# Expert layers in units of 384 tokens over two batches, with the second layer's operands swapped

## The chip, the cores and the metric

One core of a Trainium2 chip runs the kernel in one launch. The metric is the device time of that launch in microseconds; the kernel before has a median of 549.85 us over three runs (548.9 to 550.44).

## What is computed

Attention with two kinds of sparse windows over 8 batches of 576 tokens, and behind it a gated two-layer network on each batch. Everything is float32.

```python
# q, k, v: (8 batches, 8 heads, 576 tokens, 64); windows of 32 keys, heads 4..7 with every fourth key of 128
scores = q @ k.T / 8, masked;  attn = softmax(scores);  a = attn @ v
x = a as (8, 576, 512)
h = relu(x @ w_in)                              # 512 -> 1024
conv = sum over k of conv_w[k] * h[token + k - 1]   # three tokens, zero outside a batch
out = (h * sigmoid(conv)) @ w_out               # 1024 -> 512
```

The weights come in as float64 and are split in the kernel.

## The kernel before, in words

Precision is had by splitting: x, the gated h (called g) and both weights are kept as a high part and a low part, each in the type that TensorE multiplies in one go (written `F32R`), and a product is three matmuls (`TERMS`): high by high, low by high, high by low.

**Attention** (`attention`, four calls for each batch, one for each pair of heads). A call is: load q and k (tile `qk`) and v on SP's queue; scores on TensorE (L248) into the one `att` slot of PSUM; mask, maximum, subtraction on VectorE (L254, L257, L260, L262); the exponential on ScalarE (L264); sum, reciprocal, scaling and a 32x32 transpose into `pt` on VectorE (L266 to L273); the product with v on TensorE (L283), again into `att`. ScalarE copies the product into the high part of x (L320). In the first two batches TensorE subtracts it (L327, L330) and ScalarE copies the low part; later VectorE makes the low part (L335).

**Weights** (`weights`). Sixteen chunks of 512 columns and a small one for the convolution are rebuilt from the float64 words by VectorE (L430 to L441), after a first step on ScalarE (L428). Ten of the sixteen are finished by TensorE with three matmuls of 512 columns (L450 in float32, L451 and L452), the others by VectorE (L457, L463). The chunks pass through the three `out` buffers.

**The two layers** (`expert`, one call for each batch). The first layer has weights stationary and 288 tokens moving (L353): 8 chunks of 128 hidden units by 2 halves of the batch by 4 pieces of x by 3 terms, 192 matmuls. ScalarE's relu writes both halves into one `h` tile of 576 tokens and two zero columns (L360). The gating of a chunk is then one copy with the middle tap on ScalarE (L371), two taps on VectorE (L365), the sigmoid on ScalarE (L376), the product on VectorE (L378), the high part on ScalarE (L380) and the low part on VectorE (L382). There are three `h` and three `c` tiles and one `g` for each chunk. The second layer again has weights stationary and 288 tokens moving (L395), 192 matmuls, and writes the output transposed; ScalarE copies it out of PSUM (L402) and SP stores it. The host turns the result round.

**What sets the order.** `Planner` holds every piece of work as a task with an engine, a cost, what it comes after, the buffers it uses and a due time. `order()` goes through the tasks by list scheduling: on the engine that can start first, of the tasks that could start within 0.25 us the one with the earliest due time is taken. The program is then issued in that order, and each engine runs its own instructions strictly in it. Due times come from tables (`DUE`, `PAIR`, `WI`, `WO`).

Of the kernel before, what the change touches and what calls it, by code (L numbers as in the profile page):

```python
# [55 lines left out]
ONE = dict(start=True, stop=True, skip_group_check=True)  # L56

# [100 lines left out]
def attn_moe(ctx: ExitStack, tc: tile.TileContext, qk_p, qk_d, v_p, v_d, w_in, w_out, conv, mask, out):  # L158
# [10 lines left out]
    wo = [[const.tile([128, 512], F32R, name=f"wo{j}{c}") for c in range(2 * NC)] for j in range(2)]  # L169
# [172 lines left out]
    def expert(b, ready, wired, wored, conved):  # L342
        due, gated, out_due = DUE[b]
        x = [xs[b, p] for p in range(NP)]
        h, c, g = ([Buffer(n) for _ in range(NF)] for n in "hcg")
        relu = []
        for u in range(2 * NF):
            fc, hf = u // 2, u % 2
            ps, last = Buffer("nn" if b == 0 and u % 4 > 1 else "mm"), None

            def first(fc, hf, ps, k):
                for i, (jw, jx) in enumerate(TERMS):
                    nc.tensor.matmul(ps.t[:, 0:HALF], wi[jw][fc][:, k * 128:k * 128 + 128],  # L353
                                     x[k].t[jx][:, hf * HALF:hf * HALF + HALF],
                                     start=(k == 0 and i == 0), stop=(k == NC - 1 and i == 2))

            for k in range(NC):
                last = plan.add("PE", 0.396, due + 1.6 * u + 0.4 * k, lambda a=(fc, hf, ps, k): first(*a),
                                [last, wired[fc], *(ready[k] if b == 0 else sum(ready, []))], [ps, x[k]], "E")
            relu.append(plan.add("ACT", 0.4, due + 1.6 * u + 1.6, lambda fc=fc, hf=hf, ps=ps: nc.scalar.activation(  # L360
                out=h[fc].t[:, 1 + hf * HALF:1 + hf * HALF + HALF], in_=ps.t[:, 0:HALF], func=AF.Relu),
                [last], [ps, h[fc]]))

        def tap(fc, k):
            nc.vector.scalar_tensor_tensor(out=c[fc].t, in0=h[fc].t[:, k:S + k], scalar=conv_sb[:, k, fc:fc + 1],  # L365
                                           in1=c[fc].t, op0=ALU.mult, op1=ALU.add)

        gates = []
        for fc in range(NF):
            d = gated + 3.2 * fc  # L370
            t = plan.add("ACT", 0.777, d, lambda fc=fc: nc.scalar.activation(  # L371
                out=c[fc].t, in_=h[fc].t[:, 1:S + 1], func=AF.Copy, scale=conv_sb[:, 1, fc:fc + 1]),
                [relu[2 * fc], relu[2 * fc + 1], conved], [h[fc], c[fc]])
            for k in (0, 2):
                t = plan.add("DVE", 0.815, d + 0.5, lambda fc=fc, k=k: tap(fc, k), [t], [h[fc], c[fc]])
            t = plan.add("ACT", 0.686, d + 1.0, lambda fc=fc: nc.scalar.activation(  # L376
                out=c[fc].t, in_=c[fc].t, func=AF.Sigmoid), [t], [c[fc]], "sigmoid")
            t = plan.add("DVE", 0.755, d + 1.5, lambda fc=fc: nc.vector.tensor_tensor(  # L378
                out=c[fc].t, in0=c[fc].t, in1=h[fc].t[:, 1:S + 1], op=ALU.mult), [t], [c[fc], h[fc]])
            hi = plan.add("ACT", 0.675, d + 2.0, lambda fc=fc: nc.scalar.copy(out=g[fc].t[0], in_=c[fc].t),  # L380
                          [t], [c[fc], g[fc]])
            lo = plan.add("DVE", 0.755, d + 2.5, lambda fc=fc: nc.vector.tensor_tensor(  # L382
                out=g[fc].t[1], in0=c[fc].t, in1=g[fc].t[0].bitcast(F32), op=ALU.subtract), [hi], [c[fc], g[fc]])
            gates.append(lo)

        for dm in range(NC):
            o = Buffer("out")
            outs = []
            for hf in range(2):
                u = 2 * dm + hf  # L390
                ps, last = Buffer("nn"), None

                def second(dm, hf, ps, k):
                    for i, (jw, jg) in enumerate(TERMS):
                        nc.tensor.matmul(ps.t[:, 0:HALF], wo[jw][2 * dm + k // 4][:, k % 4 * 128:k % 4 * 128 + 128],  # L395
                                         g[k].t[jg][:, hf * HALF:hf * HALF + HALF],
                                         start=(k == 0 and i == 0), stop=(k == NF - 1 and i == 2))

                for k in range(NF):
                    last = plan.add("PE", 0.396, out_due + 3.3 * u + 0.4 * k, lambda a=(dm, hf, ps, k): second(*a),  # L400
                                    [last, wored[2 * dm + k // 4], gates[k]], [ps, g[k]], "E")
                outs.append(plan.add("ACT", 0.4, out_due + 3.3 + 3.3 * u, lambda hf=hf, ps=ps, o=o: nc.scalar.copy(  # L402
                    out=o.t[:, hf * HALF:hf * HALF + HALF], in_=ps.t[:, 0:HALF]), [last], [ps, o]))
                if b == B - 1:
                    plan.add("SP", 0.6, out_due + 4.0 + 3.3 * u, lambda dm=dm, hf=hf, o=o: nc.sync.dma_start(
                        out=out[b, dm, :, hf * HALF:hf * HALF + HALF], in_=o.t[:, hf * HALF:hf * HALF + HALF]),
                        [outs[-1]], [o])
            if b < B - 1:
                plan.add("SP", 1.2, out_due + 4.0 + 6.6 * dm, lambda dm=dm, o=o: nc.sync.dma_start(
                    out=out[b, dm], in_=o.t[:, :S]), outs, [o])  # L410
# [156 lines left out]
```

## Time and profile before

| what | value |
|---|---|
| median of three runs | 549.85 us (548.9 to 550.44) |
| span of the profiled execution | 549.1 us |
| mean granted clock of TensorE | 0.990 |
| last matmul ends, last ScalarE copy ends | 545.6, 546.1 us |
| TensorE, VectorE, ScalarE busy | 522.4, 415.7, 298.1 us |
| matmuls of the first and of the second layer | 1536 and 1536, 288 columns each |
| DMA, mean over the span | 95 GB/s |

In the profile PE is TensorE, PEld its weight loads, DVE VectorE, ACT ScalarE, POOL GpSimd and SP the engine that issues the transfers. A row of a group of instructions holds line, engine, operation, what it writes and reads, shapes, count, then busy time and mean duration in ns, and the idle time of the engine just before. A matmul's duration holds the time it takes to run through the array, so matmuls that follow each other overlap; what one costs is the distance between two starts. The median of the runs is 0.75 us above the profiled span.

### The profile page before, as it was taken

To read this page: it belongs to the slowest core of one execution; us is meant where nothing else is said; L and a number is where in the kernel's file an instruction comes from. 1 tells how busy PE (TensorE), PEld (TensorE's weight loads), DVE (VectorE), ACT (ScalarE), POOL (GpSimd) and SP (SyncE) were. 2 spreads that over 40 slices of the span, in tenths; PEclk is the share of its full clock that TensorE was granted. 3 is DMA by queue.
4 is the path that set the end of the run, shared out by engine and by line. 5 is a ranking of instruction groups with operands and counts; after the bars stand their busy time and mean duration, and the time that the engine had idled before them with its cause. 6 is when DMAs were issued, how large, how long until landed. Compare 5 with 4: busy or idle time off the path is not lost.

```text
span 549.1 us, 19084 instructions
## 1 busy us (share of the span) xinstructions
PE 522.4 (95%) x8664; PEld 497.2 (91%) x8664; DVE 415.7 (76%) x695; ACT 298.1 (54%) x556; POOL 0.9 (0%) x12
## 2 busy tenths in 40 slices
PE   3499978999999999999999999999999999999997
PEld 2468876999999999999999999999989999999997
DVE  4968998899997389946998389946988389946920
ACT  2457784855752486337742486237742486337721
POOL 0000000000000000000000000000000000000000
PEclk9999996999999999999999999999999999999999
DMA  7756513331044102630055102530045102300011
GB/s 247 268 157 215 195 52 137 119 121 44 7 138 152 30 23 65 200 110 23 13 161 170 32 23 72 190 113 23 17 152 162 45 23 58 117 26 23 0 44 44
DMA packets 17072, 52.31 MB, mean 95 GB/s; under 512 B 2016, under 2 KB 3168, under 8 KB 16992
## 3 DMA queue, kind: packets, MB, share of 16 engines
q1 hardware_dynamic: 16848, 51.02, 27.8%
q8 instruction: 68, 1.11, 0.9%
q10 hardware_dynamic: 144, 0.08, 0.1%
q14 instruction: 12, 0.10, 0.1%
HBM read 41.66 MB, written 9.44 MB: 93 GB/s over the span
## 4 chain that ended last, share of the span: by engine, by line
PE 92%; DVE 3%; ACT 2%; DMA 2%; issue 1%; ACTq 0%
PE nn L395 38%; PE mm L353 35%; PE att L283 8%; PE att L248 6%; PE nn L450 2%; PE nn L353 2%; PE att L327 1%; DMA qk<-in_qk_d_dram 1%; DMA qk<-in_qk_p_dram 1%; PE nn L451 0%; PE nn L452 0%; DVE pt L273 0%; DVE s L271 0%; PE att L330 0%; DVE c L365 0%
## 5 line engine op out<-in xcount | busy, mean ns | idle before, releaser
L365 DVE SCALAR_TENSOR_TENSOR c<-h,conv_sb,c 128x576 f32<-128x576 f32 x128 | 103.9, 815 | 48.4 <-ACT c L371 46.9
L360 ACT ACTIVATE h<-mm 128x288 f32<-128x288 f32 x120 | 48.8, 408 | 50.4 <-PE mm L353 50.1
L402 ACT COPY out<-nn 128x288 f32<-128x288 f32 x64 | 25.5, 400 | 70.1 <-PE nn L395 66.1
L378 DVE TENSOR_TENSOR c<-c,h 128x576 f32<-128x576 f32 x64 | 47.6, 755 | 9.4 <-ACT c L376 7.8
L283 PEld LDWEIGHTS att<-pt,v 32*64 32x64 f32 x3072 | 40.8, 138 | 14.8 <-DVE s L257 4.6
L283 PE MATMUL att<-pt,v 32*64 32x64 f32 (+2 forms) x3072 | 44.2, 232 | 9.4 <-DVE s L257 3.5
L371 ACT ACTIVATE c<-h,conv_sb 128x576 f32<-128x576 f32 x64 | 49.7, 776 | 1.3
L248 PE MATMUL att<-qk 64*32 64x64 f32 x2432 | 36.2, 235 | 11.0 <-DMA qk<-in_qk_d_dram 5.5
L248 PEld LDWEIGHTS att<-qk 64*32 64x32 f32 x2432 | 30.2, 111 | 16.9 <-DMA qk<-in_qk_d_dram 5.5
L376 ACT ACTIVATE c<-c 128x576 f32<-128x576 f32 x64 | 42.5, 678 | 2.1 <-DVE c L365 1.6
L353 PE MATMUL mm<-x2a,wi 128*128 128x288 f32 x144 | 40.5, 296 | 0.0
L353 PE MATMUL mm<-x1a,wi 128*128 128x288 f32 x144 | 40.3, 296 | 0.0
L353 PE MATMUL mm<-x3a,wi 128*128 128x288 f32 x144 | 40.3, 295 | 0.0
L353 PE MATMUL mm<-x0a,wi 128*128 128x288 f32 x144 | 40.3, 295 | 0.0
L395 PE MATMUL nn<-g2a,wo 128*128 128x288 f32 x128 | 37.0, 304 | 0.0
L395 PE MATMUL nn<-g0a,wo 128*128 128x288 f32 x128 | 36.4, 299 | 0.2
L395 PE MATMUL nn<-g6a,wo 128*128 128x288 f32 x128 | 36.6, 299 | 0.0
L395 PE MATMUL nn<-g3a,wo 128*128 128x288 f32 x128 | 36.4, 299 | 0.0
L395 PE MATMUL nn<-g1a,wo 128*128 128x288 f32 x128 | 36.4, 299 | 0.0
L395 PE MATMUL nn<-g4a,wo 128*128 128x288 f32 x128 | 36.4, 299 | 0.0
L395 PE MATMUL nn<-g5a,wo 128*128 128x288 f32 x128 | 36.4, 299 | 0.0
L395 PE MATMUL nn<-g7a,wo 128*128 128x288 f32 x128 | 36.1, 300 | 0.1
(194 smaller groups left out, 1502.5 us busy)
## 6 DMA issues: line engine op xcount, KB each, us to landing
qk<-in_qk_d_dram SPq DMA_DIRECT2D x16, 664.0 KB, 4.4
qk<-in_qk_p_dram SPq DMA_DIRECT2D x16, 592.0 KB, 4.9
out_dram<-out SPq DMA_DIRECT2D x28, 288.0 KB, 2.2
v<-in_v_d_dram SPq DMA_DIRECT2D x16, 384.0 KB, 3.4
v<-in_v_p_dram SPq DMA_DIRECT2D x16, 384.0 KB, 3.5
out<-in_w_in_dram SPq DMA_DIRECT2D x8, 512.0 KB, 4.5
out<-in_w_out_dram SPq DMA_DIRECT2D x8, 512.0 KB, 4.2
out_dram<-out SPq DMA_DIRECT2D x8, 144.0 KB, 1.8
```

Source lines behind the costliest of these rows:

```text
L248: nc.tensor.matmul(sc.t[quad * 32:quad * 32 + 32, slot // 4, slot % 4 * W:slot % 4 * W + W], q, k, start=i == 0, stop=i == len(parts) - 1, ...
L283: nc.tensor.matmul(tv.t[hd * 64:hd * 64 + 64, bank, o:o + n], v.t[quad * 32:quad * 32 + 32, block // 2, block % 2 * 64:block % 2 * 64 + 64 ...
L327: nc.tensor.matmul(tv.t[:, t, 0:128], minus, main[:, t], start=False, stop=True, skip_group_check=True)
L353: nc.tensor.matmul(ps.t[:, 0:HALF], wi[jw][fc][:, k * 128:k * 128 + 128], x[k].t[jx][:, hf * HALF:hf * HALF + HALF], start=(k == 0 and i = ...
L360: relu.append(plan.add("ACT", 0.4, due + 1.6 * u + 1.6, lambda fc=fc, hf=hf, ps=ps: nc.scalar.activation(out=h[fc].t[:, 1 + hf * HALF:1 + ...
L365: nc.vector.scalar_tensor_tensor(out=c[fc].t, in0=h[fc].t[:, k:S + k], scalar=conv_sb[:, k, fc:fc + 1], in1=c[fc].t, op0=ALU.mult, op1=ALU ...
L371: t = plan.add("ACT", 0.777, d, lambda fc=fc: nc.scalar.activation(out=c[fc].t, in_=h[fc].t[:, 1:S + 1], func=AF.Copy, scale=conv_sb[:, 1, ...
L376: t = plan.add("ACT", 0.686, d + 1.0, lambda fc=fc: nc.scalar.activation(out=c[fc].t, in_=c[fc].t, func=AF.Sigmoid), [t], [c[fc]], "sigmoid")
L378: t = plan.add("DVE", 0.755, d + 1.5, lambda fc=fc: nc.vector.tensor_tensor(out=c[fc].t, in0=c[fc].t, in1=h[fc].t[:, 1:S + 1], op=ALU.mult ...
L395: nc.tensor.matmul(ps.t[:, 0:HALF], wo[jw][2 * dm + k // 4][:, k % 4 * 128:k % 4 * 128 + 128], g[k].t[jg][:, hf * HALF:hf * HALF + HALF], ...
L402: outs.append(plan.add("ACT", 0.4, out_due + 3.3 + 3.3 * u, lambda hf=hf, ps=ps, o=o: nc.scalar.copy(out=o.t[:, hf * HALF:hf * HALF + HALF ...
L450: nc.tensor.matmul(ps.t, ident, t(), start=True, stop=False)
```

## The change

The unit of the two layers is no longer a batch but 384 tokens: two batches of 576 tokens are three units, each of two segments of 192. x of both batches now lies in one tile for each pair of heads, the two batches side by side with zero columns before, between and behind (`xt`), instead of seven rotating buffers.

The first layer's moving operand is a window of two runs of 194 columns, a segment with a neighbour at each side, so 388 columns and no halves; relu writes both runs into `h` at once, and the neighbours are computed twice. The gating works on two runs of 192. There are 12 `g` buffers instead of 8, each of 384 tokens.

In the second layer g is stationary, 128 tokens at a time, and the weights move, 512 columns; the output comes out with tokens in rows, 36 stores of 128 rows. `w_out` is laid out by 128 hidden units instead of by output columns. GpSimd's memsets write the zero columns of x, 24 instead of 6.

All due times are new: a table `DUE` of its own for each unit, pair of heads and weight chunk. Costs of the planner's tasks follow the new shapes.

```diff
+UNITS = 3
+SEG, SEGS = S // 3, 2
+HALO = SEG + 2
+UNIT = SEGS * SEG
+XB = S + 1
+XW = 2 * XB + 2
...
+DUE = {
+    "first": (-267.74, -248.77, 696.14, -362.32, 670.22, 937.38, 948.43, 1088.83, 1172.91, 1498.80, 1690.92, 1705.61),
...
+}
...
-    slots("x", 7, [128, S], F32R, 2)
-    slots("g", NF, [128, S], F32R, 2)
-    hs = slots("h", 3, [128, S + 2])
-    slots("c", 3, [128, S])
+    xt = [[const.tile([128, XW], F32R, name=f"x{p}{'ab'[j]}") for j in range(2)] for p in range(NP)]
+    for p in range(NP):
+        for odd in range(2):
+            plan.pool(f"x{p}{odd}", [[t[:, 1 + odd * XB:1 + odd * XB + S] for t in xt[p]]])
+    slots("g", 12, [128, UNIT], F32R, 2)
+    slots("h", 3, [128, SEGS, HALO])
+    slots("c", 3, [128, SEGS, SEG])
...
+        def window(t):
+            at = [(s // 3) * XB + s % 3 * SEG for s in (part * SEGS, part * SEGS + 1)]
+            t = t[:, at[0]:at[1] + HALO]
+            return bass.AP(t.tensor, t.offset, [t.ap[0], [at[1] - at[0], SEGS], [1, HALO]])
...
-                    nc.tensor.matmul(ps.t[:, 0:HALF], wi[jw][fc][:, k * 128:k * 128 + 128],
-                                     x[k].t[jx][:, hf * HALF:hf * HALF + HALF],
+                    nc.tensor.matmul(ps.t[:, 0:SEGS * HALO], wi[jw][fc][:, k * 128:k * 128 + 128], window(xt[k][jx]),
                                      start=(k == 0 and i == 0), stop=(k == NC - 1 and i == 2))
...
-                last = plan.add("PE", 0.396, due + 1.6 * u + 0.4 * k, lambda a=(fc, hf, ps, k): first(*a),
+                last = plan.add("PE", 0.493, first_due + 1.97 * fc + 0.49 * k, lambda a=(fc, ps, k): first(*a),
...
-                        nc.tensor.matmul(ps.t[:, 0:HALF], wo[jw][2 * dm + k // 4][:, k % 4 * 128:k % 4 * 128 + 128],
-                                         g[k].t[jg][:, hf * HALF:hf * HALF + HALF],
-                                         start=(k == 0 and i == 0), stop=(k == NF - 1 and i == 2))
+                    nc.tensor.matmul(ps.t, g[k].t[jg][:, j * 128:j * 128 + 128], wo[jw][k],
+                                     start=(k == 0 and i == 0), stop=(k == NF - 1 and i == 2))
...
-                    last = plan.add("PE", 0.396, out_due + 3.3 * u + 0.4 * k, lambda a=(dm, hf, ps, k): second(*a),
+                last = plan.add("PE", 0.648, out_due + 5.2 * j + 0.65 * k, lambda a=(j, ps, k): second(*a),
...
-    for h, in hs:
-        nc.gpsimd.memset(h[:, 0:1], 0.0)
-        nc.gpsimd.memset(h[:, S + 1:S + 2], 0.0)
+    for p in range(NP):
+        for t in xt[p]:
+            for i in range(3):
+                nc.gpsimd.memset(t[:, i * XB:i * XB + 1].bitcast(F32), 0.0)
...
-        "w_out": w_out.reshape(2, 4, 128, NC, 128).transpose(3, 0, 2, 1, 4).reshape(2 * NC, 128, 512),
+        "w_out": w_out.reshape(NF, 128, DM),
```

In the changed kernel the lines are: scores L261, masks to transpose L267 to L286, product with v L296, subtraction on TensorE L340 and L343, low part of x on VectorE L348, first layer L373, taps L384, product L398, low part of g L402, second layer L411, weight splits L441 to L474 on VectorE and L461 to L463 on TensorE.

Where the instructions moved is seen at the ninth attention. First TensorE's order before around the ninth product with v (its rows end in the instruction's written shape); 384 matmuls of the first layer and 264 of the second stand ahead of it:

```order
L395 MATMUL nn_163<-g6a,wo_93 128x288
L395 MATMUL nn_163<-g7a,wo_85 128x288
L395 MATMUL nn_163<-g7b,wo_85 128x288
L395 MATMUL nn_163<-g7a,wo_93 128x288
L283 MATMUL att_159<-pt_112,v_102 64x32 x8
L283 MATMUL att_159<-pt_112,v_102 64x64 x24
L283 MATMUL att_159<-pt_112,v_102 64x32 x16
L395 MATMUL nn_162<-g0a,wo_84 128x288
```

That is the second layer of the second batch in full flow. In the changed kernel the same place in TensorE's order, with 252 matmuls of the first layer and 78 of the second ahead of it:

```order
L373 MATMUL mm_162<-x3a,wi_78 128x388
L411 MATMUL nn_164<-wo_82,g8a 128x512
L411 MATMUL nn_164<-wo_82,g8b 128x512
L411 MATMUL nn_164<-wo_90,g8a 128x512
L411 MATMUL nn_164<-wo_83,g9a 128x512
L411 MATMUL nn_164<-wo_83,g9b 128x512
L411 MATMUL nn_164<-wo_91,g9a 128x512
L296 MATMUL att_161<-pt_112,v_102 64x64 x24
L296 MATMUL att_161<-pt_112,v_102 64x32 x8
L296 MATMUL att_161<-pt_112,v_102 64x16 x16
L411 MATMUL nn_164<-wo_84,g10a 128x512
```

The ninth product now stands in the second unit's second layer, whose g8 and g9 come from gatings just ahead in VectorE's order. Eight products with v, eleven score blocks and ten weight splits stand ahead in both. VectorE's order before, up to the ninth transpose:

```order
L382 TENSOR_TENSOR g6b<-c_149,g6a 128x576
L378 TENSOR_TENSOR c_147<-c_147,h_144 128x576
L254 TENSOR_TENSOR s_103<-att_159,mask_sb 128x512
L382 TENSOR_TENSOR g7b<-c_147,g7a 128x576
L257 TENSOR_TENSOR s_103<-att_159,mask_sb 128x64
L260 TENSOR_REDUCE m_106<-s_103 128x9
L266 TENSOR_REDUCE z_111<-s_105 128x9
L268 TENSOR_SCALAR z_111<-z_111 128x9
L270 RECIPROCAL z_111<-z_111 128x9
L271 TENSOR_TENSOR s_105<-s_105,z_111 128x576
L273 STREAM_TRANSPOSE pt_112<-s_105 128x576
```

Sixteen gatings of 576 tokens are done by then, two batches' worth. VectorE's order in the changed kernel, up to the same transpose:

```order
L267 TENSOR_TENSOR s_103<-att_161,mask_sb 128x512
L402 TENSOR_TENSOR g3b<-c_149,g3a 128x384
L270 TENSOR_TENSOR s_103<-att_161,mask_sb 128x64
L273 TENSOR_REDUCE m_106<-s_103 128x9
L275 TENSOR_TENSOR s_103<-s_103,m_106 128x576
L267 TENSOR_TENSOR s_104<-att_161,mask_sb 128x512
L270 TENSOR_TENSOR s_104<-att_161,mask_sb 128x64
L273 TENSOR_REDUCE m_107<-s_104 128x9
L279 TENSOR_REDUCE z_111<-s_105 128x9
L281 TENSOR_SCALAR z_111<-z_111 128x9
L283 RECIPROCAL z_111<-z_111 128x9
L284 TENSOR_TENSOR s_105<-s_105,z_111 128x576
```

Again sixteen gatings are done, but of 384 tokens, and one more score block has been taken in.

More of the change, by code (lines that the diff above doesn't have):

```diff
@@ L346, in expert, with first @@
         relu = []
[L347 to L351, printed above, removed]
+        for fc in range(NF):
+            ps, last = Buffer("nn" if u == 0 and fc % 2 else "mm"), None
+            def first(fc, ps, k):
                 for i, (jw, jx) in enumerate(TERMS):
-                    nc.tensor.matmul(ps.t[:, 0:HALF], wi[jw][fc][:, k * 128:k * 128 + 128],
-                                     x[k].t[jx][:, hf * HALF:hf * HALF + HALF],
+                    nc.tensor.matmul(ps.t[:, 0:SEGS * HALO], wi[jw][fc][:, k * 128:k * 128 + 128], window(xt[k][jx]),
@@ L355, in first @@
                                      start=(k == 0 and i == 0), stop=(k == NC - 1 and i == 2))
             for k in range(NC):
-                last = plan.add("PE", 0.396, due + 1.6 * u + 0.4 * k, lambda a=(fc, hf, ps, k): first(*a),
[L359 to L362, printed above, removed]
+                last = plan.add("PE", 0.493, first_due + 1.97 * fc + 0.49 * k, lambda a=(fc, ps, k): first(*a),
+                                [last, wired[fc], *(t for b in used for t in (ready[b][k] if u == 0 else sum(ready[b], [])))],
+                                [ps, *x[k]], "E")
@@ L364, in tap @@
+            relu.append(plan.add("ACT", 0.49, first_due + 1.97 * fc + 1.97, lambda fc=fc, ps=ps: nc.scalar.activation(
+                out=h[fc].t.rearrange("p a k -> p (a k)"), in_=ps.t[:, 0:SEGS * HALO], func=AF.Relu), [last], [ps, h[fc]]))
         def tap(fc, k):
-            nc.vector.scalar_tensor_tensor(out=c[fc].t, in0=h[fc].t[:, k:S + k], scalar=conv_sb[:, k, fc:fc + 1],
+            nc.vector.scalar_tensor_tensor(out=c[fc].t, in0=h[fc].t[:, :, k:k + SEG], scalar=conv_sb[:, k, fc:fc + 1],
@@ L366, in tap @@
                                            in1=c[fc].t, op0=ALU.mult, op1=ALU.add)
+        split = lambda t: t.rearrange("p (a k) -> p a k", a=SEGS)
         gates = []
         for fc in range(NF):
[L370 to L373, printed above, removed]
+            d = gated + 1.97 * fc
+            t = plan.add("ACT", 0.617, d, lambda fc=fc: nc.scalar.activation(
+                out=c[fc].t, in_=h[fc].t[:, :, 1:SEG + 1], func=AF.Copy, scale=conv_sb[:, 1, fc:fc + 1]),
+                [relu[fc], conved], [h[fc], c[fc]])
@@ new lines, in expert, with second @@
+            gates.append(plan.add("DVE", 0.557, d + 2.5, lambda fc=fc: nc.vector.tensor_tensor(
+                out=split(g[fc].t[1]), in0=c[fc].t, in1=split(g[fc].t[0].bitcast(F32)), op=ALU.subtract),
+                [hi], [c[fc], g[fc]]))
+        for j in range(UNIT // 128):
+            o, ps, last = Buffer("out"), Buffer("nn"), None
+            def second(j, ps, k):
+                for i, (jw, jg) in enumerate(TERMS):
+                    nc.tensor.matmul(ps.t, g[k].t[jg][:, j * 128:j * 128 + 128], wo[jw][k],
+                                     start=(k == 0 and i == 0), stop=(k == NF - 1 and i == 2))
+            for k in range(NF):
+                last = plan.add("PE", 0.648, out_due + 5.2 * j + 0.65 * k, lambda a=(j, ps, k): second(*a),
+                                [last, wored[k], gates[k]], [ps, g[k]], "E")
+            row = u * UNIT + j * 128
+            last = plan.add("ACT", 0.587, out_due + 5.2 * j + 5.2, lambda ps=ps, o=o: nc.scalar.copy(
+                out=o.t[:, 0:DM], in_=ps.t), [last], [ps, o])
+            plan.add("SP", 1.0, out_due + 5.2 * j + 6.0, lambda row=row, o=o: nc.sync.dma_start(
+                out=out[row:row + 128], in_=o.t[:, 0:DM]), [last], [o])
```

74 lines of the change are left out of this document (27 added, 47 removed).

## The prediction

> **What bounds the kernel now.** I read the page first (busy shares and the chain that ended last), then the windows, the chain in order of time, the timeline of TensorE (PE) and VectorE (DVE), and the groups by line.
>
> ```profile
> span 549.1 us, 19084 instructions
> ...
> PE 522.4 (95%) x8664; PEld 497.2 (91%) x8664; DVE 415.7 (76%) x695; ACT 298.1 (54%) x556; POOL 0.9 (0%) x12
> ...
> PE 92%; DVE 3%; ACT 2%; DMA 2%; issue 1%; ACTq 0%
> ```
>
> PE is busy nearly all the time and 92% of the last chain is PE's own work. That is the average over two stages, though, and the windows (columns: length, then busy of PE, PEld, DVE, ACT, POOL, then granted clock) part them at 161.25 us, the start of the ninth product of probabilities and values (L283), which I call V9.
>
> ```profile
> 0.00:161.25 161.25, 139.27 (x2344) 126.07 (x2347) 140.47 (x255) 98.23 (x181) 0.90 (x12) 0.97 0.41 142
> 161.25:545.60 384.35, 383.18 (x6328) 371.11 (x6328) 275.20 (x441) 199.51 (x374) 0.00 (x0) 1.00 0.24 76
> ```
>
> After V9 PE idles 1.2 of 384.35 us; the end is then V9's time plus PE's work. Before V9 PE idles 22 us and VectorE is busy 140 of 161 us: it splits the weights, runs the softmaxes and the first gatings. Its ninth transpose and V9 stand close together (timeline of VectorE, then a piece of the chain):
>
> ```profile
> 158.69 0.78 DVE L273 STREAM_TRANSPOSE pt<-s 128x576 f32<-128x576 f32 x1
> ```
> ```profile
> 161.25 1.19 PE att L283 x77
> ```
>
> The transpose ends at 159.47, V9 starts 1.8 us later. So the sum has two terms: when VectorE lets V9 start, and how much PE work is left behind V9. The profiled span of 549.1 lies 0.75 under the median of the runs, 549.85; differences are worked out on the span's trace and put on the median.
>
> **PE's price of a matmul.** The chain has long unbroken runs of the two layers:
>
> ```profile
> 316.54 16.30 PE mm L353 x123
> ...
> 526.24 19.36 PE nn L395 x144
> ```
>
> 16.30/123 is 132.5 ns for 288 columns (19.36/144 is 134 with one start). All 3072 of them make 407 us. For 512 columns of the same type the trace has one place, the third matmul of a weight split (L452). Its price is the distance to the next start:
>
> ```profile
> 67.69 0.39 PE L452 MATMUL nn<-wi,minus 128*128 128x512 f32 x1
> 67.92 0.29 PE L353 MATMUL nn<-x0a,wi 128*128 128x288 f32 x1
> ...
> 70.67 0.39 PE L452 MATMUL nn<-wi,minus 128*128 128x512 f32 x1
> 70.90 0.30 PE L353 MATMUL nn<-x1a,wi 128*128 128x288 f32 x1
> ```
> ```profile
> 90.58 0.63 PE L452 MATMUL nn<-wo,minus 128*128 128x512 f32 x1
> 91.00 0.52 PE L327 MATMUL att<-x6a,minus 128*128 128x128 f32 x2
> ```
> ```profile
> 88.30:91.80 3.50, 3.50 (x11) 2.27 (x9) 3.33 (x7) 2.19 (x4) 0.00 (x0) 0.50 0.69 238
> ```
>
> At full clock 230 ns; at a granted clock of 0.50 it is 420, which halved is 210, or 0.410 ns per column. So at full clock something above the bare columns is paid: 20 ns at 512, and 132.5-118 = 14.5 ns at 288. High end for the new widths: the line through (288, 132.5) and (512, 230), which gives 176 ns at 388. Low end of that reading: 14.5 ns per matmul whatever the width, 173.6 at 388 and 224.5 at 512. I take 175 and 227, nearer to neither. The first layer goes from 1536 to 1152 matmuls, the second from 1536 to 864: 1152x0.175+864x0.227 = 397.7 against 407. The wider columns therefore save only some 9 us over the whole run, since first-layer columns grow by 1% and the second layer's stay equal.
>
> The first layer now reads two runs of 194 columns. No row has that, but the subtraction matmuls read contiguous columns of x1 in one batch and every fourth column of x2:
>
> ```profile
> L327 PE MATMUL att<-x1a,minus x8: 223/276/300, 33.0 to 98.2; 128*128 128x128 f32 x8
> ...
> L327 PE MATMUL att<-x2a,minus x4: 274/274/296, 36.6 to 36.9; 128*128 128x128 f32 x4
> ```
>
> 276 and 274 in the median: a step in the columns costs nothing there. I take 0; these rows bound it by 2 ns either way, 2 us over the run.
>
> **VectorE up to V9.** By the order of the instructions VectorE has the same work in front of the ninth transpose in both kernels: nine softmaxes, 16 weight chunks, conv and masks, and 16 gatings of four instructions (two L365, L378, L382). Only the gatings' width changes, 576 to 384, and one more score block (L254, L257, L260, L262) stands ahead.
>
> ```profile
> L365 DVE SCALAR_TENSOR_TENSOR c<-h,conv_sb,c 128x576 f32<-128x576 f32 x128 | 103.9, 815 | 48.4 <-ACT c L371 46.9
> L378 DVE TENSOR_TENSOR c<-c,h 128x576 f32<-128x576 f32 x64 | 47.6, 755 | 9.4 <-ACT c L376 7.8
> ...
> L262 DVE TENSOR_TENSOR s<-s,m 128x576 f32<-128x576 f32 x32 | 24.1, 753 | 0.7
> L260 DVE TENSOR_REDUCE m<-s 128x9 f32<-128x576 f32 x32 | 24.0, 751 | 0.8
> L254 DVE TENSOR_TENSOR s<-att,mask_sb 128x512 f32<-128x512 f32 x32 | 21.8, 680 | 2.4 <-PE att L248 2.3
> ...
> L257 DVE TENSOR_TENSOR s<-att,mask_sb 128x64 f32<-128x64 f32 x32 | 6.6, 208 | 0.0
> L382 DVE TENSOR_TENSOR g7b<-c,g7a 128x576 fp32r<-128x576 f32 x8 | 6.1, 758 | 1.7 <-ACT g7a L380 0.7
> ...
> L463 DVE TENSOR_TENSOR wo<-w1b,wo 128x512 fp32r<-128x512 f32 x3 | 2.1, 688 | 0.0
> ```
>
> 512 against 576 wide is 688 against 755-758, 1.05 ns per column, so 192 fewer columns save 0.20: 64x0.20 = 12.9 us. The score block costs 0.68+0.21+0.75+0.75 = 2.4. VectorE comes to the ninth transpose 10.5 us sooner, at 149.0, and V9 to 149.2, 12.0 sooner, if PE is there. It is: ahead of V9 it had 648 layer matmuls, 85.9 us, and now 252 of 388 and 78 of 512 columns, 44.1+17.7 = 61.8, with the same eight products, eleven score blocks and ten weight splits. PE loses 24 us of work ahead of V9 and V9 comes only 12 sooner: PE idles some 12 us more.
>
> **Behind V9.** Left were 2424 matmuls, 321.2 us; now 900x0.175+786x0.227 = 157.5+178.4 = 335.9, 14.7 more. The other PE work behind V9 is the same. Sum: -12.0+14.7 = +2.7.
>
> The rest. ScalarE loads its tables 24 times instead of 16, and copies 36 outputs of 512 instead of 64 of 288; the last copy and the last transfer grow:
>
> ```profile
> L402 ACT COPY out<-nn 128x288 f32<-128x288 f32 x64 | 25.5, 400 | 70.1 <-PE nn L395 66.1 <-issue 1.4 <-DVE w1a L441 1.4
> L376 ACT ACT_TABLE_LOAD x8 | 10.3, 1283 | 0.1
> ...
> L455 ACT CAST wi<-nn 128x512 fp32r<-128x512 f32 x8 | 4.7, 584 | 6.1 <-PE nn L452 6.0
> ```
> ```profile
> out_dram<-out SPq DMA_DIRECT2D x28, 288.0 KB, 2.2
> ...
> out_dram<-out SPq DMA_DIRECT2D x8, 144.0 KB, 1.8
> ```
>
> Eight loads are 10 us on an engine that is busy 54%; PE's queue ahead hides them, and uncovered each would cost 1.3. The tail grows by 0.2 (584 for 400) and up to 0.4 (2.2 for 1.8): +0.6. POOL's 18 further memsets stand between the two steps that make `ident`; POOL is busy 0.9 us in all for 12 instructions and `ident` is first used by PE well behind the first scores, so nothing. SP's loads change order, and bytes stay the same but for the outputs' packing; nothing waits for SP behind V9 in the before trace, and ahead of it VectorE sets the pace. Total +3.3: 549.85+3.3 = 553.
>
> **Rivals.** First, faster: the excess over the bare columns belongs to the short matmul (its weights are loaded while it runs, and a longer one covers the load), so that 388 and 512 columns cost 0.159 and 0.210. For it: 210 at half the clock's rate, and that every full-clock row of 512 stands directly behind float32 matmuls (L450), so no steady stream of them is in the trace. Against: those rows agree on 230. The second term becomes 900x0.159+786x0.210-321.2 = -13.0, and with -12.0+0.6 the time would be 525; but VectorE then has, behind V9, 275.2+80x2.34-48x3.14-2.4 = 309 us in 371, and at 87% busy ahead of V9 it made PE idle, so I add 8: 533. It decides where the steady distance of L411 is under 0.218. The Trainium skill's page "TensorE: Matmul & The Clock Gate", section "Back-to-back issue gap", has N/2.4+2.5 ns at full clock, and the traces speak against it, 132.5 here for its 122.5 and 230 for its 215.8; by it the second term would be -3.8 and the time 535.
>
> Second, no change: VectorE fills its early waits. It stood for ScalarE's first step of a weight chunk (waits: total us, times, longest):
>
> ```profile
> DVE w0a L430 <- ACT w0a L428: 3.6, 4, 1.1
> ...
> DVE w1a L430 <- ACT w1a L428: 1.2, 1, 1.2
> ```
>
> The new order mixes chunks and softmaxes from the first instruction; if all 4.8 go, V9 comes at 144.4 and the time is 548.5. Against it: the chunks' three buffers still make each load wait for the chunk three before.
>
> Third, slower still: behind V9 VectorE has no slack for a while, since two units' gatings and five softmaxes come before PE has a stock; each us that it waits there is PE's too, up to 3 on top, and with the high end of the matmul price (0.176 and 0.230, +3.3) the time is 559.
>
> **How the numbers follow.** The forecast (V9 set by VectorE, 175 and 227 ns) with its own range 549 to 559 has a chance of 0.5, the third rival in it; the first rival 0.36; the second 0.14. A measurement of this kernel tells 0.3%, 1.65 us. The forecast is slower in 0.45 and within that in 0.05; the first rival is faster in 0.36; the second is faster in 0.04, same in 0.06, slower in 0.04. Faster 0.40, same 0.11, slower 0.49. The range runs from 533 to 559, since the first rival holds too much to be left out.
>
> **What would show it.** Right: L411 in unbroken runs at 0.225 to 0.230 per matmul and L373 at 0.173 to 0.177; the ninth product of L296 at 147 to 152 us; PE idle ahead of it 30 to 38 us; behind it near nothing. Wrong: L411 at 0.216 or less (first rival), V9 before 146 (second), or PE idle of several us behind V9 with VectorE as the releaser (third).

## The result, and the profile after

The changed kernel takes 556.36 us in the median of four runs (555.59 to 556.88), against 549.92 for the kernel before beside it (548.9 to 550.44): a ratio of 1.0113, with a 95% interval of 1.0091 to 1.0134. It is 6.4 us slower; 3.3 were forecast. The page of the changed kernel, its span, its busy shares and the shares of its last chain:

```profile
span 554.4 us, 17170 instructions
...
PE 519.5 (94%) x7608; PEld 451.3 (81%) x7608; DVE 434.6 (78%) x823; ACT 318.7 (57%) x600; POOL 1.5 (0%) x30
...
PE 83%; DVE 11%; ACT 3%; issue 1%; DMA 1%; SPq 0%; DVEq 0%; ACTq 0%
```

PE has 2.9 us less to do (522.4 before) and yet the end comes later: PE's share of the last chain fell from 92% to 83%, VectorE's rose from 3% to 11%. PE waits more. Split at V9, the ninth product (L296), which now starts at 150.86 us (windows, columns as in the prediction):

```profile
0.00:150.86 150.86, 119.85 (x2027) 98.92 (x2027) 131.34 (x257) 83.50 (x162) 1.50 (x30) 0.91 0.43 147
150.86:550.78 399.92, 399.62 (x5583) 352.38 (x5582) 303.25 (x567) 234.62 (x437) 0.00 (x0) 1.00 0.22 74
```

Behind V9 PE idles 0.3 us: the end is still V9's time plus PE's work. Ahead of V9 PE idles 31.0 us, 9.0 more than before. Where these lie, windows by stage show, first of the kernel before:

```profile
0.00:45.00 45.00, 27.71 (x756) 22.29 (x757) 32.63 (x73) 20.02 (x38) 0.90 (x12) 1.00 0.67 231
45.00:83.00 38.00, 35.03 (x682) 31.31 (x681) 36.73 (x66) 29.11 (x54) 0.00 (x0) 1.00 0.39 135
83.00:115.00 32.00, 30.42 (x441) 27.39 (x431) 27.88 (x49) 21.82 (x41) 0.00 (x0) 0.84 0.38 129
115.00:150.00 35.00, 35.00 (x330) 34.69 (x329) 32.80 (x52) 21.05 (x41) 0.00 (x0) 1.00 0.13 47
```

and of the changed kernel:

```profile
0.00:45.00 45.00, 26.84 (x613) 16.29 (x614) 37.87 (x81) 20.75 (x37) 1.50 (x30) 0.89 0.70 247
45.00:83.00 38.00, 27.99 (x807) 23.60 (x792) 31.45 (x60) 17.15 (x35) 0.00 (x0) 0.82 0.53 171
83.00:115.00 32.00, 32.00 (x332) 29.74 (x333) 30.11 (x59) 24.92 (x52) 0.00 (x0) 1.00 0.22 79
115.00:150.00 35.00, 32.17 (x298) 28.88 (x297) 31.09 (x59) 20.68 (x40) 0.00 (x0) 0.95 0.18 59
```

Between 45 and 83 us PE's idle time goes from 3.0 to 10.0 us; that is most of the 9. What PE waited for there (total us, times, longest) is spread over many short waits:

```profile
PE att L296 <- DVE s L270: 1.3, 1, 1.3
PE att L340 <- ACT x2a L333: 1.3, 1, 1.3
PE att L261 <- DVE s L270: 1.3, 1, 1.3
PE att L296 <- ACT x2b L346: 1.3, 1, 1.3
PE att L296 <- issue: 1.2, 1, 1.2
PE att L261 <- ACT x1b L346: 0.8, 1, 0.8
...
```

With four more rows behind ScalarE's copies (2.8 us) that is 6.2 us behind copies of an attention's product, 2.6 us behind the last mask step of a score block and 1.2 us behind nothing that the profile shows. The first matmul of the first layer starts at 67.3 us, where it was 35.7. From 83 us on PE is busy without a break except for 2.8 us, and VectorE, too, is busy 30 of the 32 us up to 115. The ninth transpose (timeline of VectorE):

```profile
149.24 0.78 DVE L286 STREAM_TRANSPOSE pt<-s 128x576 f32<-128x576 f32 x1
```

It ends at 150.02, 1.0 later than forecast, and V9 starts 0.8 behind it. The one stop, in the chain that ended last:

```profile
120.04 0.63 ACT wo L473
...
120.69 0.69 DVE wo L474
121.38 0.14 DVE s L270
...
121.57 0.97 PE att L261 x58
...
134.15 3.43 PE nn L411 x15
137.58 6.41 PE mm L373 x36
```

PE had stopped at 118.74. Its next scores (L261) need the attention buffer, which the last step of a score block (L270) frees, and that stands behind steps of weight chunks in VectorE's queue. The last rows are PE's prices: 6.41/36 is 178 ns for 388 columns, 3.43/15 is 228.7 for 512.

### The profile page after: what moved, and what is told of

Read it like the earlier page. It is cut to its first block, busy times and chain, and to the rows that moved or that the text cites. A ratio compares the mean times of both kernels' runs of the same rounds, so it can differ in the third digit from the quotient of the medians.

```text
span 554.4 us, 17170 instructions
## 1 busy us (share of the span) xinstructions
PE 519.5 (94%) x7608; PEld 451.3 (81%) x7608; DVE 434.6 (78%) x823; ACT 318.7 (57%) x600; POOL 1.5 (0%) x30
## 4 chain that ended last, share of the span: by engine, by line
PE 83%; DVE 11%; ACT 3%; issue 1%; DMA 1%; SPq 0%; DVEq 0%; ACTq 0%
PE nn L411 35%; PE mm L373 34%; PE att L296 7%; PE att L261 5%; DVE c L384 1%; PE nn L373 1%; DVE r L452 1%; DVE w0b L446 1%; DMA qk<-in_qk_d_dram 1%; DVE m L273 1%; DVE s L267 1%; PE att L340 1%; DVE s L275 1%; DVE c L398 1%; DVE w1b L446 1%
## 5 line engine op out<-in xcount | busy, mean ns | idle before, releaser
L384 DVE SCALAR_TENSOR_TENSOR c<-h,conv_sb,c 128x384 f32<-128x384 f32 x192 | 116.7, 616 | 26.5 <-ACT c L391 23.8
L380 ACT ACTIVATE h<-mm 128x388 f32<-128x388 f32 x92 | 45.1, 492 | 46.0 <-PE mm L373 43.7
L391 ACT ACTIVATE c<-h,conv_sb 128x384 f32<-128x384 f32 x96 | 58.6, 615 | 9.3 <-DVE g4b L402 5.3
L373 PE MATMUL mm<-x0a,wi 128*128 128x388 f32 x184 | 63.6, 345 | 0.0
L373 PE MATMUL mm<-x1a,wi 128*128 128x388 f32 x184 | 63.2, 343 | 0.0
L373 PE MATMUL mm<-x2a,wi 128*128 128x388 f32 x184 | 63.1, 343 | 0.0
L373 PE MATMUL mm<-x3a,wi 128*128 128x388 f32 x184 | 62.9, 342 | 0.0
L398 DVE TENSOR_TENSOR c<-c,h 128x384 f32<-128x384 f32 x96 | 52.1, 555 | 12.0 <-ACT c L396 10.6
L396 ACT ACTIVATE c<-c 128x384 f32<-128x384 f32 x96 | 48.5, 520 | 6.6 <-DVE c L384 6.0
L296 PEld LDWEIGHTS att<-pt,v 32*64 32x64 f32 x3072 | 39.8, 134 | 14.6 <-issue 4.9
L261 PEld LDWEIGHTS att<-qk 64*32 64x32 f32 x2432 | 29.9, 111 | 24.0 <-issue 5.8
L261 PE MATMUL att<-qk 64*32 64x64 f32 x2432 | 35.3, 235 | 14.6 <-DMA qk<-in_qk_d_dram 7.6
L296 PE MATMUL att<-pt,v 32*64 32x64 f32 (+2 forms) x3072 | 43.5, 228 | 4.2 <-issue 1.5
L373 PEld LDWEIGHTS mm<-x0a,wi 128*128 128x128 f32 x184 | 34.7, 189 | 1.5
L373 PEld LDWEIGHTS mm<-x2a,wi 128*128 128x128 f32 x184 | 35.0, 190 | 0.2
L373 PEld LDWEIGHTS mm<-x1a,wi 128*128 128x128 f32 x184 | 34.8, 189 | 0.3
L373 PEld LDWEIGHTS mm<-x3a,wi 128*128 128x128 f32 x184 | 34.6, 188 | 0.1
L373 PE MATMUL mm<-x3b,wi 128*128 128x388 f32 x92 | 31.4, 341 | 0.4 <-ACT x3b L346 0.4
L373 PE MATMUL mm<-x2b,wi 128*128 128x388 f32 x92 | 31.5, 342 | 0.0
L373 PE MATMUL mm<-x1b,wi 128*128 128x388 f32 x92 | 31.3, 340 | 0.0
```

What stands on the lines that cost most here:

```text
L261: nc.tensor.matmul(sc.t[quad * 32:quad * 32 + 32, slot // 4, slot % 4 * W:slot % 4 * W + W], q, k, start=i == 0, stop=i == len(parts) - 1, ...
L296: nc.tensor.matmul(tv.t[hd * 64:hd * 64 + 64, bank, o:o + n], v.t[quad * 32:quad * 32 + 32, block // 2, block % 2 * 64:block % 2 * 64 + 64 ...
L373: nc.tensor.matmul(ps.t[:, 0:SEGS * HALO], wi[jw][fc][:, k * 128:k * 128 + 128], window(xt[k][jx]), start=(k == 0 and i == 0), stop=(k == ...
L380: relu.append(plan.add("ACT", 0.49, first_due + 1.97 * fc + 1.97, lambda fc=fc, ps=ps: nc.scalar.activation(out=h[fc].t.rearrange("p a k - ...
L384: nc.vector.scalar_tensor_tensor(out=c[fc].t, in0=h[fc].t[:, :, k:k + SEG], scalar=conv_sb[:, k, fc:fc + 1], in1=c[fc].t, op0=ALU.mult, op ...
L391: t = plan.add("ACT", 0.617, d, lambda fc=fc: nc.scalar.activation(out=c[fc].t, in_=h[fc].t[:, :, 1:SEG + 1], func=AF.Copy, scale=conv_sb[ ...
```

## The experiments

**The price of a matmul.** e1_widths is the changed kernel with nine runs of 48 matmuls behind the last store.

```diff
+        for i in range(48):
+            nc.tensor.matmul(probe[:, 0:388], word(i), move(i, 388), **ONE)
... (the same with 128, 192, 256, 288, 448, 512 columns, with two runs of 194, and with one weight tile and 512)
```

> The changed kernel with nine runs of 48 matmuls put behind its last store, when the other engines are quiet: first-layer weights against x at 128, 192, 256, 288, 388, 448 and 512 contiguous columns, once 388 columns in two runs of 194, and 512 columns with one and the same weight piece. Theory (about 13 ns are added to each matmul whatever its width, and the two runs cost some 4 ns more): 288 at 132.5 ns from start to start, 388 contiguous at 174 to 175, 388 in two runs at 178, 448 at 199 to 200, 512 at 226 to 227, so 0.417 ns for a further column; below some 230 columns the distance stops falling, near 111. Rival 1 of the prediction (a long matmul covers the cost): 388 at 162 to 165 and 512 at 214 to 216. Rival (a slower rate per column, the line the prediction drew as its high end): 388 at 176 to 178 in both forms, 448 at 202 to 203, 512 at 229 to 230.

Its chain, in which a run is one piece (L505 128 columns, L507 192, L511 288, L513 388 in one run, L515 388 in two, L519 512, L521 512 with the same operands each time):

```profile
550.25 5.31 PE mm L505 x48
555.56 5.39 PE mm L507 x48
...
566.69 6.36 PE mm L511 x48
573.05 8.44 PE mm L513 x48
581.49 8.56 PE mm L515 x48
...
599.72 11.10 PE mm L519 x48
610.82 10.93 PE mm L521 x48
```

132.5 ns at 288, 175.8 at 388, 178.3 at 388 in two runs, 231.3 at 512, 227.7 with operands that stay. What the bare columns cost can be estimated from the changed kernel behind the stop at 118.7 us, where the granted clock is 0.50 (a piece of PE's timeline, then the window):

```profile
124.34 0.63 PE L411 MATMUL nn<-wo,g7b 128*128 128x512 f32 x1
124.77 0.63 PE L411 MATMUL nn<-wo,g7a 128*128 128x512 f32 x1
```
```profile
124.30:125.20 0.90, 0.90 (x4) 0.64 (x2) 0.51 (x2) 0.87 (x2) 0.00 (x0) 0.50 0.79 326
```

The starts lie 427 ns apart there (0.43 in the rows). If a column's time goes with the granted clock, it is at most 0.417 ns at full clock, which is 120, 161.8 and 213.5 ns for 288, 388 and 512. The excess over them is 12.5, 14.0 (16.5 with two runs) and 17.8 ns: it does not vanish with the width, as the first rival would have it, and it is not the constant 13 of e1's theory either; 288, 388 and 512 lie nearest to the prediction's high end, 132.5, 176 and 230. e4_contig asks what the two runs cost in place:

```diff
-            t = t[:, at[0]:at[1] + HALO]
-            return bass.AP(t.tensor, t.offset, [t.ap[0], [at[1] - at[0], SEGS], [1, HALO]])
+            at = min(at[0], XW - 1 - SEGS * HALO)
+            return t[:, at:at + SEGS * HALO]
```

> The changed kernel with the first layer reading 388 contiguous columns instead of two runs of 194 (the second segment's columns are then the wrong ones; all sizes stay). Theory (the two runs cost about 4 ns a matmul): first-layer matmuls at 174 to 175 ns instead of 178, the time lower by 1152 x 4 = 3 to 4.5 us. Rival (the 178 ns are the price of 388 columns beside busy engines): 177 to 179 ns and no change of the time, within 1 us.

556.12 us (554.46 to 557.39), 1.0108 (1.0079 to 1.0136) of the kernel before; L373 at 176.8 ns from start to start in unbroken runs, against 178.3 in the changed kernel. Two runs cost 1.5 (e4) to 2.5 ns (e1), at most 2.9 us over 1152 matmuls, and not the 4 ns that both expectations had as their theory; in the time nothing of it shows.

**VectorE's sum of work.** The prediction let V9 start when VectorE had done its sum. Three kernels take work from VectorE in different places.

```diff
 # e2_taps_first (e3_taps_late: u == 6)
         def tap(fc, k):
+            if u == 0:
+                return
 ...
 # e6_narrow_in: for the chunks of w_in, 8 of 512 columns at L441, L446 and L449; L441 is shown
-            out=u(), in0=u(), scalar1=2.0 ** -15,
+            out=some(u()), in0=some(u()), scalar1=2.0 ** -15,
```

> The changed kernel without the 16 taps of the first unit on VectorE (this leaves out two of the three convolution terms for the first 384 tokens): 16 x 0.616 = 9.9 us of VectorE's work ahead of the ninth product is gone. Theory (VectorE's work sets when V9 starts, and behind V9 PE is the bound): V9 comes 7 to 10 us earlier than 150.9 and the time falls by as much, to 546.5 to 549.5. Rival (loads, the single score slot or ScalarE set the start): V9 and the time move by less than 2 us.

> The changed kernel without the 16 taps of the seventh unit (this leaves out two of the three convolution terms for 384 tokens in the middle): the same 9.9 us of VectorE's work, but behind V9. Theory (behind V9 PE alone sets the pace): no change, within 1 us of 556.4. Rival (VectorE sets the pace all through, so that the change is slower because VectorE has 23 us more to do): 547 to 550.

> Leaves out most of three VectorE steps of the eight w_in chunks (8 of 512 columns; the weights are wrong), in an unchanged order: about 9 us less VectorE work in the first 60 us. Theory of the prediction, VectorE's sum of work lets the ninth product (V9) start: V9 from 150.9 to about 142, time about 548. Rival, a chain of round trips through one attention buffer (scores on PE, softmax on VectorE and ScalarE, product on PE, copies on ScalarE) sets the pace up to 83 us, with VectorE's chunks filling its gaps: V9 moves by 0 to 3 us, time 553 to 556.

e2: 558.89 us (1.0156, 1.0129 to 1.0184), V9 at 151.4. e3: 557.69 (1.0141, 1.0113 to 1.0169). e6: 556.59 (1.0125, 1.0089 to 1.0160), V9 at 150.3. How far V9 moves by itself from one execution to the next is seen in e1, e3 and e4, which have the same work ahead of it as the changed kernel: 150.3, 151.8 and 151.0 us, beside 150.9. VectorE's busy time by the pages is 8.4 us less in e2 and 8.1 less in e6; the theory of the prediction wanted V9 some 8 us sooner in both and falls in both, since neither moves V9 out of that scatter of 1.5 us. That e2 and e3 come out 2.5 and 1.3 us above the changed kernel was not expected and stays unexplained; their intervals overlap its own. Windows of e2, the stage from which the taps were taken:

```profile
83.00:115.00 32.00, 31.64 (x331) 29.15 (x330) 21.80 (x42) 25.48 (x53) 0.00 (x0) 1.00 0.24 80
```

VectorE has 8.3 us less to do here than in the changed kernel and PE is as busy as it was: from 83 us on PE itself sets the pace. The first two stages of e6:

```profile
0.00:45.00 45.00, 28.97 (x640) 18.72 (x640) 31.10 (x82) 21.05 (x38) 1.50 (x30) 0.92 0.72 250
45.00:83.00 38.00, 27.67 (x757) 23.58 (x758) 30.82 (x59) 16.55 (x34) 0.00 (x0) 0.82 0.56 173
```

6.8 us less VectorE work up to 45 us, and PE idles in the second stage as before (10.3). Ahead of 83 us something other than the sum holds.

**The order, or what stands in it?** e5_batch0_first lets the first layer begin early by due times alone.

```diff
-    "pair": ((-379.84, -334.82, -577.81, -300.28),
+    "pair": ((-479.84, -434.82, -677.81, -400.28),
-    "wi": (-459.96, -481.83,
+    "wi": (-759.96, -781.83,
```

> The same work in another order: batch 0's four softmaxes and the first two chunks of the first layer's weights come first, so that the first layer can start long before 67 us. Theory 'late start': the changed kernel idles 10 us of PE between 45 and 83 us (3 before) because its order lets the first layer begin at 67 us instead of 36. Then the first layer's matmul (L373) starts at about 36, that idle falls to about 3 us, and the time is 549 to 551. Theory 'small unit': VectorE does as much before PE has a stock (76.2 of the first 90 us in both kernels), but a unit of 384 tokens of one batch gives PE a third less work than a batch of 576, and the second unit needs batch 1 too. Then L373 starts early and PE runs dry again: 8 us or more of further idle between 45 and 150, and the time is 563 to 575.

574.42 us, 1.0438 (1.0410 to 1.0466). L373 starts at 34.8 us, as wanted, and PE runs dry (windows):

```profile
45.00:83.00 38.00, 21.90 (x677) 19.52 (x664) 20.60 (x39) 9.97 (x20) 0.00 (x0) 0.59 0.40 126
83.00:115.00 32.00, 30.75 (x299) 26.91 (x300) 23.98 (x47) 25.81 (x53) 0.00 (x0) 0.87 0.25 84
```

PE idles 16.1 of 38 us in the second stage. "Late start" falls: of the two orders tried, the one with the late first layer is the better for such units. The reason given, that the second unit needs batch 1, is then tested by itself in the kernel before:

```diff
 # e9_before_couple, on the kernel before; nxt: batch 1's results, for batch 0
-    slots("v", 3, [128, NV, 128])
+    slots("v", 2, [128, NV, 128])
-    slots("x", 7, [128, S], F32R, 2)
+    slots("x", 8, [128, S], F32R, 2)
...
-                                [last, wired[fc], *(ready[k] if b == 0 else sum(ready, []))], [ps, x[k]], "E")
+                                [last, wired[fc], *(ready[k] if b == 0 else sum(ready, [])), *(nxt if hf else ())], [ps, x[k]], "E")
```

> The kernel before, with one wait added: the first layer of batch 0's second half waits for batch 1's softmaxes too, as the changed kernel's second unit does (eight x buffers in place of seven and two v buffers in place of three, to make room). Widths, matmuls and due times stay. Theory 'coupling': this wait alone takes from PE, between 45 and 150 us, the work that fills its gaps; with due times that put batch 0 first PE idles 15 to 25 us more there and the time is 565 to 575, as in the changed kernel with batch 0 first. Rival, the early idle comes from the narrower gatings and the new widths: PE has enough other work, and the time stays within 2 us of 550.

573.59 us, 1.0432 (1.0397 to 1.0467), with every width as before, as its theory had it. Its windows:

```profile
45.00:83.00 38.00, 22.07 (x757) 19.05 (x763) 34.54 (x67) 11.58 (x24) 0.00 (x0) 0.74 0.55 182
83.00:115.00 32.00, 26.51 (x437) 23.89 (x426) 17.88 (x27) 20.51 (x37) 0.00 (x0) 0.78 0.20 65
```

and what PE waited for between 45 and 83 us (total us, times, longest):

```profile
PE att L248 <- DVE s L257: 11.2, 3, 4.4
PE att L283 <- DVE s L257: 3.1, 1, 3.1
```

PE's idle time in the second stage is 15.9 us, with that one wait, against 3.0 without; over the run it is 42.3 against 23.1. While batch 1's attentions go through the one attention buffer, scores wait for the score block ahead, and the first layer's matmuls, which filled those gaps, are held back. The planner orders the program anew with the wait in it, so other instructions moved too. Of the two buffer counts that had to change to make room, the fewer v buffers are not what PE waits for: no wait of PE for a load of v stands in the profile. The waits are those of e5, where 11.0 of the 16.1 us are waits of scores and products for the last mask step (L270); in the changed kernel itself most are short waits for ScalarE's copies. What e9 shows is that in the kernel before the wait for batch 1 takes away the work that fills such waits; for the changed kernel that is carried over, not measured.

**The one stop at 118.7 us.** e8_narrow_out is e6's edit for the chunks of w_out.

> Leaves out most of three VectorE steps of the eight w_out chunks (the weights are wrong), in an unchanged order: some 5 us less VectorE work between 105 and 121 us. Theory 'order of VectorE': PE idles 2.8 us at 118.7 since its next scores wait for a score block's add (L270) that stands behind these chunks in VectorE's queue; the idle goes, V9 comes 2.5 to 3 us sooner, the time is 553 to 554. Rival, that add waits for something else: the idle stays, time 555.5 to 557.

555.32 us (553.78 to 556.07), 1.0088 (1.0060 to 1.0117). Windows of e8:

```profile
115.00:125.00 10.00, 9.47 (x109) 7.32 (x108) 9.42 (x20) 2.52 (x5) 0.00 (x0) 1.00 0.09 18
```

The stop is gone (PE 9.47 where it had 7.17, and no idle stretch over 0.6 us stands there), so VectorE's queue caused it. V9 came only 0.9 sooner, at 149.9, which is less than it scatters by. In the profiled execution the first layer began late, at 70.3 us, and that start varies from one execution to the next (67.3 in the changed kernel, 68.2 to 69.3 in e1, e3 and e4, which have the same work up to there); between it and V9 lie 79.6 us, where those four have 81.0 to 83.6.

**The clock.** e7_warm gives PE 132 matmuls that nobody reads, ahead of the first layer.

```diff
... (mms are the first layer's two PSUM buffers)
+        busy = iter((17, 19, 0, 9, 0, 0, 0, 2, 10, 6, 0, 14, 9, 0, 0, 5, 0, 0, 9, 9, 9, 9, 0, 0, 5))
         for t in plan.order():
             t.run()
+            for _ in range(next(busy, 0) if t.engine == "PE" else 0):
+                nc.tensor.matmul(mms[0][0][:, 0:128], minus, minus, **ONE)
```

> The changed kernel with matmuls of 128 columns that nobody reads put into PE's idle stretches ahead of the first layer, so that PE hardly rests there. Theory 'clock': the granted clock between 20 and 80 us (0.5 to 0.7 in several stretches of 5 us, where the kernel before has 1.00) lengthens the chain; with the clock near 1.00 there V9 comes 3 to 5 us sooner and the time is 551 to 553. Rival, the clock lies beside the waits: V9 within 1.5 us of 150.9, time 555 to 558.

560.80 us (557.58 to 562.37), 1.0184 (1.0144 to 1.0224), V9 at 154.0. Both expectations missed. The clock was 0.98 up to 45 us (0.89 in the changed kernel) and 0.85 in the second stage (0.82), and PE's idle ahead of V9 fell to 16.6 us, but PE had 22.6 us of matmuls more to run. The better clock and the added work can't be told apart by this run; what a full clock alone would bring stays open.

**Round trips and VectorE together.** Each attention of the first two batches takes the attention buffer twice: for the scores, until VectorE's mask steps have read them, and for the product, through ScalarE's copies and PE's subtraction. A piece of the changed kernel's chain shows such a round trip, with the finish of a weight chunk (L461) in PE's queue behind it:

```profile
56.35 1.21 ACT x2a L333 x2
...
57.60 1.12 PE att L340 x4
58.72 0.36 PE att L343 x2
...
59.10 1.21 ACT x2b L346 x2
...
60.36 1.87 PE att L296 x80
62.23 2.01 PE nn L461 x2
```

e10 shortens VectorE's softmax steps, which lie between the two holds, e11 the end of the second hold on PE and ScalarE, e12 does both.

```diff
 # e10_soft (some = 8 if b < 2 else W), so at L273, L275, L279, L284
-            out=m.t, in_=s.t, axis=AX.X, op=ALU.max), [last], [s, m])
+            out=m.t, in_=s.t[:, :, 0:some], axis=AX.X, op=ALU.max), [last], [s, m])
 # e11_tail
-                for t in range(4):
-                    nc.tensor.matmul(tv.t[:, t, 0:128], minus, main[:, t], start=False, stop=True,
...
-                for g in range(2):
-                    nc.tensor.matmul(src(1)[:, g], minus, rest[:, g], start=False, stop=True, skip_group_check=True)
+                nc.tensor.matmul(tv.t[:, 0, 0:8], minus, main[:, 0, 0:8], start=False, stop=True,
...
-            ... lambda i=i: nc.scalar.copy(out=parts(x.t[1])[i], in_=src(i)),
+            ... lambda i=i: nc.scalar.copy(out=parts(x.t[1])[i][..., 0:8], in_=src(i)[..., 0:8]),
...
+        nc.gpsimd.memset(xt[p][1].bitcast(F32), 0.0)
```

The memsets, one for each pair of heads, are GpSimd's (busy 5.5 us in place of 1.5).

> The changed kernel with four of the nine VectorE steps of each softmax of batches 0 and 1 cut to 8 of 64 columns (results wrong), in an unchanged order: about 2.4 us less of VectorE's work per softmax, 19 us ahead of 85 us, and shorter round trips by as much. Theory 'two chains': VectorE's work and the round trips through the one attention buffer (PE, VectorE, ScalarE) are equally long there, so that cutting into one alone brings little: V9 1 to 4 us sooner, time 553 to 555. Theory of the prediction (VectorE's sum): V9 15 us or more sooner, time about 541.

> The changed kernel with the end of each attention of batches 0 and 1 cut short (the subtraction on PE one matmul of 8 columns, ScalarE's copies of x1 8 columns; x1 is wrong), in an unchanged order: each hold of the attention buffer is some 1.2 us shorter, VectorE's work is the same. Theory 'two chains': VectorE holds the pace, V9 0 to 2 us sooner, time 554.5 to 556.5. Rival, the attention buffer alone sets the pace: V9 7 to 10 us sooner, time 547 to 549.

> Both cuts together. Theory 'two chains': more than the sum of the two, V9 6 to 10 us sooner, time 547 to 550. Rival, a third thing (loads, or PE's own work) sets the pace ahead of 83 us: V9 within 3 us, time 553 or more.

| kernel | time, us | ratio to before (interval) | first layer starts, us | V9, us | PE's own work and its idle time ahead of V9 |
|---|---|---|---|---|---|
| changed | 556.36 | 1.0113 (1.0091, 1.0134) | 67.3 | 150.9 | 119.8 and 31.0 |
| e10_soft | 555.69 | 1.0122 (1.0082, 1.0162) | 66.7 | 149.7 | 121.3 and 28.4 |
| e11_tail | 552.04 | 1.0041 (1.0025, 1.0057) | 63.9 | 146.5 | 115.1 and 31.4 |
| e12_soft_tail | 543.67 | 0.9886 (0.9872, 0.9901) | 58.6 | 138.1 | 110.3 and 27.9 |

V9 moves by 1.2, 4.3 and 12.7 us. The first is less than V9 scatters by, though VectorE has 16.6 us less to do, and both cuts bring far more than the sum of the two, more than e12's theory had: so it is with two paths of nearly equal length, where cutting one leaves the other. The chains that end where the first layer starts say the same. In the changed kernel VectorE has 36.3 of the chain's 67 us and PE 13.8; in e1, e3 and e4, with the same work up to there, VectorE's part is anything from 23.3 to 33.4. In e6 the two have 17.4 and 25.8, in e10 12.2 and 33.2, and the first layer starts at 66.8 and 66.7 us all the same. The path through PE is not the attentions alone: 14.9 of its 33.2 us in e10 are weight splits (L462 to L464 there), as in this piece of e10's chain:

```profile
37.67 1.13 PE att L261 x65
38.81 2.00 PE nn L462 x2
40.81 0.43 PE nn L463
41.24 0.43 PE nn L464
41.66 1.42 PE att L297 x79
```

e11 lies between its two expectations. Read as two paths, the one through PE is the longer by some 4 us, with VectorE's right behind. The second stage, first e11, then e12:

```profile
45.00:83.00 38.00, 29.78 (x832) 24.16 (x833) 33.97 (x66) 14.81 (x38) 0.00 (x0) 0.73 0.57 177
```
```profile
45.00:83.00 38.00, 31.28 (x801) 27.70 (x804) 28.64 (x69) 19.77 (x48) 0.00 (x0) 0.87 0.54 172
```

In e11 VectorE fills up (33.97 for 31.45 us); with its steps cut as well it has 28.64 and the first layer starts at 58.6 us instead of 67.3.

Two things besides the paths are in these numbers. The matmuls of the subtraction left out were 5.6 us of PE's work ahead of V9, more than e11's whole gain, and e11's idle time did not fall. And in e12 PE's work is 9.6 us less: the 4.0 us beyond the 5.6 are the same matmuls in less time, at a mean granted clock of 0.96 up to V9 in place of 0.91. Only 3.1 of e12's 12.7 us are idle time. How much of the gain beyond the sum is the paths' and how much the clock's, no run parts. e12 leaves work out, so it is no kernel to use; no version here that does all the work beats the kernel before.

## Why the forecast was right in direction and half the size

| term, us | forecast | measured |
|---|---|---|
| V9 sooner | -12.0 | -10.3 (161.2 to 150.9) |
| from V9 to PE's last matmul | +14.7 | +15.5 (384.4 to 399.9) |
| tail | +0.6 | +0.1 (3.53 to 3.64) |
| span | +3.3 | +5.3 |
| place of the profiled span before in its runs | 0 | +1.1 |
| median | +3.3 (553) | +6.4 |

The forecast is 3.1 us short: 1.7 at V9, 0.8 behind it and 1.1 in the level, less 0.5 in the tail.

**V9.** The step that failed is "VectorE comes to the ninth transpose 10.5 us sooner, at 149.0, and V9 to 149.2 [...] if PE is there. It is". The number was 1.7 us off, the ground under it was wrong. VectorE's sum alone is not what V9 waits for: 8.1 to 16.6 us less of it brought V9 forward by 1.2 us at most (e2, e6, e10), where it scatters over 1.5 us by itself. V9 comes when PE gets to it. Up to the first layer's start PE depends on a path of round trips through the attention buffer, with weight splits between them, and on VectorE's sum close beside it (e10, e11, e12). It has little to put into the gaps; that a unit which spans two batches holds its matmuls back is shown in the kernel before (e9), and e5's early start fits it. From 83 us on PE works through its queue, with one stop of 2.8 us that VectorE's order makes (e8). That the sum came so near is luck: the two paths happen to be of like length. How much of the 9.0 us of further idle time each of these causes has, and what the lower granted clock ahead of V9 (0.91, 0.97 before) adds, stays open. The prediction did see that PE would have less work ahead of V9 and idle more (12 us; 9.0 measured) but took the idle time for a remainder, not for a cost that another unit would not have.

**Behind V9.** 175 and 227 ns were near; in unbroken runs it is 178.3 (the prediction's sign said 173 to 177) and 228.5, and 900x0.1783+786x0.2285 = 340.1 is 4.2 us over the 335.9 forecast. Two things nearly cancel it. Added up in the traces, from each start to the next start or its own end, the layers behind V9 took 332.0 us before where 321.2 were counted and take 349.1 now: what lies between the unbroken runs, where attentions break in, took 10.8 us before and 9.0 now, 1.8 less. The attentions themselves and PE's idle time came to 1.6 less. What is left is +0.8. That the two runs cost nothing was wrong by 1.5 to 2.5 ns, about the bound given; the rows of 128 columns that were read for it hold durations of 274 and 276 ns, not distances between starts, and could not show so little.

**The level.** In all four runs of the changed kernel the time is 1.8 us above the span, and in 23 runs of the kernel before whose span is on record 1.74 to 1.89. By that the profiled execution before took some 550.9 us, 1.1 above its median, so a difference between the two traces put on that median falls 1.1 short. This is worked out, not measured: none of the four runs beside the result is that long. The 0.75 in the prediction mixed two executions.

**The rivals.** The first (long matmuls at 0.159 and 0.210) fails: 512 columns cost 228.5, above the 218 from which it decides. The Trainium skill, "TensorE: Matmul & The Clock Gate", section "Back-to-back issue gap", has N/2.4+2.5 ns, 215.8 at 512 columns, for a matmul by itself and, for a stream with weight loads, some 131 ns at 512; no run here agrees with either, 231.3 with new weights each time and 227.7 with the same ones. The second (V9 before 146) and the third (PE waiting for VectorE behind V9) did not come: PE idles 0.3 us there and e3, which spares VectorE work behind V9, gains nothing.

## What to carry to other kernels

An engine that is 87% busy ahead of a point need not be what that point waits for: take its work away in the trace's own order and see whether the next stage moves, and look for a path through several engines and one buffer beside it. Before a small move is read as an effect, see how far the point moves by itself in runs that do the same work. Units that need two producers' results can cost the work that used to fill the gaps at the start; count what can start after the first producer. And compare a trace with the runs by its own execution's time, or the level is off by as much as a term.

## What was not expected of the hardware

- A matmul with a weight load of its own takes 110.6 ns at 128 columns and 112.3 at 192 (e1), nearly the same; from 288 columns on it is the bare columns (0.417 ns each, the estimate above) plus 12 to 18 ns. Moving columns in two runs cost 2.5 ns, and new operands each time 3.6 ns at 512.
- The granted clock had a mean of 0.59 in e5 between 45 and 83 us, where PE idled 16.1 us, and the same matmuls ahead of V9 took 128.4 us of PE instead of 119.8. That idle time brings the clock down is not shown: the kernel before idled 17.3 us of its first 45 at a granted clock of 1.00.
